# Row maxima of an attention layer: the queue from which their transfers are issued

## The chip, the cores and the metric

The kernel runs on one core of one Trainium2 chip. The metric is device time in microseconds (us), the median of several executions. Lower is better. A core has TensorE (matmuls; PE in the profile, with its weight loads as PEld), VectorE (DVE), ScalarE (ACT), GpSimd (POOL) and SyncE (SP). Each has a queue of its own that it works off in order. A transfer (DMA) is issued by an instruction in one of these queues and then carried out by 16 DMA engines.

## The reference

Four layers on a sequence of 2048 rows of 640 numbers: attention, Fourier mixing, attention, Fourier mixing, each with a layer norm ahead and a residual added.

```python
def _A_ref(x, wqkv, wo):
    B, S, D = x.shape
    H = 32; Dh = D // H; W = 256
    qkv = (lambda x, *d: x.transpose(*d))((x @ wqkv).reshape(B, S, 3, H, Dh), 2, 0, 3, 1, 4)
    q, k, v = qkv[0], qkv[1], qkv[2]
    scores = jnp.einsum("bhqd,bhkd->bhqk", q, k) * (Dh ** -0.5)
    idx = jnp.arange(S)
    mask = (idx[:, None] - idx[None, :] >= 0) & (idx[:, None] - idx[None, :] < W)
    scores = jnp.where(mask[None, None], scores, -1e9)
    p = _softmax(scores, axis=-1)
    o = jnp.einsum("bhqk,bhkd->bhqd", p, v)
    return (lambda x, *d: x.transpose(*d))(o, 0, 2, 1, 3).reshape(B, S, D) @ wo
...
x = x + _A_ref(_layernorm(x, axis=-1), A_wqkv, A_wo)
x = x + _B_ref(_layernorm(x, axis=-1), B_dft_seq_re, B_dft_seq_im, B_dft_hid_re, B_dft_hid_im)
x = x + _A_ref(_layernorm(x, axis=-1), A_wqkv, A_wo)
x = x + _B_ref(_layernorm(x, axis=-1), B_dft_seq_re, B_dft_seq_im, B_dft_hid_re, B_dft_hid_im)
```

Only the attention layers bear on the change: 32 heads of 20 numbers, each query attending to itself and the 255 keys before it.

## The kernel before, in words

The heads of a layer are worked off in eight quads of four heads. A quad has 16 blocks of 128 queries or keys, so the loop `heads` takes 8 x 16 = 128 steps, with 10 more ahead (`LEAD`). A step is made of two half steps (`z` = 0 and 1), each for two heads.

The scores are computed twice, in two orientations:

- Ahead, at step `s = t + 10`, queries stand on the partitions (`s_head`, matmul at L673). VectorE adds the mask and takes each row's maximum (L678), which goes to a small tile `mc`.
- At step `t`, keys stand on the partitions (`t_pair`, matmul at L701), so that the exponentials (`t_exp`, ScalarE, L711, into `pt`) can be multiplied with the values directly. In this orientation a row's maximum can't be subtracted by a per-partition number. It is carried by the matmul itself instead: row 60 (and row 124 for the other head of the pair) of the query tile `qp` holds minus the maximum, against a row of ones in `kp`. GpSimd then sets the masked probabilities to zero (L717, L721).

The product with the values (`pv`, L736) follows a step later, and ScalarE copies it out (L745).

Every fourth step, `m_rows` brings the maxima of four query blocks into place. I call one such unit a row block; there are 4 in a quad, 32 in a layer, 64 in the two attention layers. TensorE transposes `mc` (L686) in the second half step. ScalarE copies the result with its sign turned into `mt` (L689). Two transfers of 4 KB in all (L691), one for each `z`, write rows 60 and 124 of `qp`. The matmuls at L701 of four steps on are the first to read them. `mt` has one buffer.

The order of work is written out by hand. Every call adds an instruction to the queue of its engine, and the queue keeps that order. `post(delay, fn)` puts off a call by `delay` half steps; `tick`, at the end of every half step, makes the calls that have become due. With a delay of 1 a call is made in the tick that ends the half step in which it was posted. After the copy at L689 a half step of the steady loop adds nothing more to ScalarE's queue before that tick, and the next half step begins with its own L701 matmuls, scores (L673) and exponential (L711). In the ten steps ahead, matmuls of the projection stand between, with ScalarE's copies of their results (L586).

All transfers of the kernel are issued by SyncE (SP). In the heads these are, besides the row maxima: the parts of `qp` and `kp` for the next quad (`pack`, L636), the projected pieces to memory (`store_qk`, L566), the values (`load_v`, L663), the outputs and the sums of the probabilities (`finish`: `sm` and `o_d` at L755 and L756, `r_d` at L761), a check of the Fourier matrices (loads at L1458, a square on ScalarE at L1469), and weights.

PSUM has eight banks. The scores of both orientations, the transposed maxima and the products with the values share banks 0 to 5 by a plan made ahead (`borrow`, `borrow_pair`, with times in `AT_T`, `AT_S`, `HELD_T` and so on): a bank that an exponential empties in one half step is taken by a score matmul of the next. The matmuls between, at L274, are the projection and the output product (`fill`), a fixed number in each step.

Of the kernel before, what the change touches and what calls it, by code (L numbers as in the profile page):

```python
# [73 lines left out]
class Net:  # L74
# [573 lines left out]
    def heads(self, xsrc, xdst):  # L648
        nc = self.nc
# [33 lines left out]
        def m_rows(quad, u, bank):  # L683
            m = mc.pop((quad, u))
            p = self.banks[:16, bank, 3 * P:]
            nc.tensor.transpose(p, m.rearrange("p z e j -> p (z e j)"), self.ident)  # L686
            mt = pool.tile([16, P], F32R, name="mt", tag="mt", bufs=1)
            yield
            nc.scalar.activation(mt, p, AF.Copy, scale=-1.0)  # L689
            for z in range(2):  # L690
                self.post(1, lambda z=z: nc.sync.dma_start(  # L691
                    qp[quad % 2][60:125:64, z, u * 512:(u + 1) * 512].bitcast(F32),
                    mt[8 * z:8 * z + 8, :].bitcast(F32)))

# [123 lines left out]
        for step in range(-LEAD, steps + 1):  # L818
# [27 lines left out]
            for z in range(2):  # L846
                if 0 <= t < steps:
                    banks = self.borrow_pair(clock + AT_T[z], HELD_T)
                    t_pair(t // 16, t % 16, z, banks)
                if 0 <= s < steps:  # L850
                    for e, b in enumerate(self.borrow(clock + AT_S[z], *HELD_S)):
                        s_head(s // 16, s % 16, 2 * z + e, b)
                if z and (rows or 0 <= v < steps):
                    last, = self.borrow(clock + AT_PV, HELD_PV)
                m = m_rows(*rows, last) if z and rows else iter(())
                next(m, None)
                if 0 <= t < steps:
                    t_exp(t // 16, t % 16, z, banks)
                    t_mask(t // 16, t % 16, z)
                if self.heavy:  # L860
                    self.heavy.sort(key=lambda h: h[0] not in ROLES["m"])
                    self.relieve()
                if z:
                    if 0 <= v < steps:
                        pv(v // 16, v % 16, last)
                    for _ in m:
                        pass
                if z == 0 or t < -1 or t >= steps:
                    fill(nf)
                self.tick()  # L870
# [813 lines left out]
```

## Time and profile before

| | |
|---|---|
| median of 3 runs | 1386.3 us |
| lowest, highest | 1385.91, 1390.49 us |
| profiled execution | 1394.17 us, span 1391.8 us |
| mean granted clock of TensorE | 0.983 |
| PE busy | 1303.8 us (94%) |
| DVE busy | 965.4 us (69%) |
| ACT busy | 758.4 us (54%) |
| POOL busy | 722.3 us (52%) |
| DMA moved | 261.48 MB |

Times in the profile are counted from the start of the span. Busy times are of the one profiled execution and don't add up, since the engines work side by side. Issuing a transfer isn't counted as busy time. In a row of the timeline the first number is the start, the second the length; "x2" means two instructions merged into one row; in square brackets stands how long the engine was idle before it, and what ended that. In a row of the waits stand the total, the count and the longest. A row of a source line has the shortest, median and longest duration in ns. SPq is SyncE's queue. The first attention layer's heads run from some 147 to 530 us, the second's from some 833 to 1236.

### The profile page before, as it was taken

What the parts mean: (1) busy time and instruction counts of PE and PEld (TensorE: products, weight loads), DVE (VectorE), ACT (ScalarE), POOL (GpSimd) and SP (SyncE); (2) the same over time, 40 slices, a digit from 0 to 9 for tenths busy, and PEclk for the clock granted to TensorE, in tenths of its full rate; (3) what the DMA queues carried; (4) which work ended last, traced back from release to release, by engine and by line L of the source; (5) the groups of instructions that cost most, each with busy time, mean ns of one, the idle gap of its engine ahead of it and who ended that gap; (6) DMA issues with size and microseconds to landing.
All of it is one profiled execution on the core that took longest, in us unless ns stands there. A gap on an engine that the chain in (4) does not pass through costs nothing.

```text
span 1391.8 us, 37371 instructions
## 1 busy us (share of the span) xinstructions
PE 1303.8 (94%) x13350; PEld 1002.5 (72%) x13350; DVE 965.4 (69%) x3124; ACT 758.4 (54%) x1651; POOL 722.3 (52%) x1501
## 2 busy tenths in 40 slices
PE   6998999999998989899999999999999989999997
PEld 6898777767766767753689987777677667777445
DVE  6722788778877774777866238888688778658664
ACT  3222378767776555437422224777677755644450
POOL 4211687768777655320322136887778766733000
PEclk9999999999999999999999999999999999999999
DMA  5675567777668874617425646777776777653443
GB/s 193 206 220 168 166 204 214 203 214 213 202 207 220 234 207 134 199 54 242 171 93 184 216 151 196 216 195 224 196 225 191 235 231 209 207 157 108 140 127 144
DMA packets 174295, 261.48 MB, mean 188 GB/s; under 512 B 36306, under 2 KB 85586, under 8 KB 174100
## 3 DMA queue, kind: packets, MB, share of 16 engines
q1 hardware_dynamic: 174100, 259.00, 61.8%
q8 instruction: 108, 1.77, 0.6%
q14 instruction: 87, 0.71, 0.2%
HBM read 175.42 MB, written 82.31 MB: 185 GB/s over the span
## 4 chain that ended last, share of the span: by engine, by line
PE 36%; DMA 5%; POOL 3%; DVE 3%; issue 3%; ACT 2%; SPq 0%; POOLq 0%; ACTq 0%; DVEq 0%
PE banks L274 8%; PE banks L256 7%; PE banks L736 5%; PE banks L701 4%; PE banks L1382 3%; PE banks L673 3%; PE banks L1298 3%; PE banks L1398 1%; DMA sm<-ou 1%; ACT pt L711 1%; DMA qp<-mt 1%; DVE banks L678 1%; POOL pt L717 1%; DMA big<-x_d 1%; PE banks L362 1%
## 5 line engine op out<-in xcount | busy, mean ns | idle before, releaser
L678 DVE CUSTOM_DVE_ANT_0 banks<-banks,mask 128x384 f32<-128x384 f32 (+2 forms) x1024 | 526.8, 556 | 135.7 <-PE banks L673 115.7
L711 ACT ACTIVATE pt<-banks 128x768 f32<-128x768 f32 (+2 forms) x512 | 393.7, 770 | 162.0 <-PE banks L701 116.0
L717 POOL TENSOR_SCALAR_AFFINE_SELECT pt<-pt 128x256 f32<-128x256 f32 x512 | 218.9, 428 | 172.7 <-ACT pt L711 144.8
L274 PE MATMUL banks<-big,wc 64*128 64x512 f32 x1920 | 278.7, 400 | 0.4 <-DVE pt L480 0.4
L701 PE MATMUL banks<-qp,kp 61*128 61x384 f32 (+2 forms) x1024 | 211.0, 382 | 36.0 <-DVE mc L678 20.9
L673 PE MATMUL banks<-kp,qp 60*128 60x384 f32 (+2 forms) x1024 | 212.4, 356 | 13.3 <-DVE mc L678 9.3
L736 PE MATMUL banks<-pt,vq 128*32 128x128 f32 x5760 | 215.4, 281 | 1.2 <-ACT pt L711 0.8
L274 PEld LDWEIGHTS banks<-big,wc 64*128 64x128 f32 x1920 | 194.4, 189 | 20.4 <-ACT x L586 2.8
L721 POOL TENSOR_SCALAR_AFFINE_SELECT pt<-pt 128x256 f32<-128x256 f32 x448 | 185.9, 415 | 0.0
L736 PEld LDWEIGHTS banks<-pt,vq 128*32 128x32 f32 x5760 | 144.4, 111 | 51.7 <-issue 37.2
L701 PEld LDWEIGHTS banks<-qp,kp 61*128 61x128 f32 x1024 | 109.0, 186 | 100.6 <-DVE mc L678 71.2
L673 PEld LDWEIGHTS banks<-kp,qp 60*128 60x128 f32 x1024 | 126.0, 189 | 42.2 <-DVE mc L678 25.5
L678 DVE DVE_READ_ACCUMULATOR2_ANT mc<- 128x1 f32 x1024 | 143.6, 140 | 0.0
L1465 POOL TENSOR_TENSOR rr<-rr 128x228 f32<-128x228 f32 (+3 forms) x113 | 74.9, 667 | 87.4 <-DMA rr<-ki 34.6
L745 ACT ACTIVATE ou<-banks 128x128 f32<-128x128 f32 (+2 forms) x288 | 73.2, 266 | 66.7 <-PE banks L736 62.3
L256 PE MATMUL banks<-qp,big 128*128 128x320 f32 x576 | 99.9, 319 | 1.0 <-POOL qp L382 1.0
L228 POOL TENSOR_TENSOR c<-x,c 128x256 fp32r<-128x256 f32 x128 | 94.8, 748 | 0.0
L256 PEld LDWEIGHTS banks<-qp,big 128*128 128x128 f32 x576 | 89.8, 194 | 1.6 <-POOL qp L382 1.4
L256 PE MATMUL banks<-qp,kp 128*128 128x320 f32 x384 | 82.2, 347 | 6.9 <-ACT big L1118 4.5
L274 PE MATMUL banks<-big,big 64*128 64x320 f32 x912 | 79.6, 310 | 0.2 <-ACT mt L689 0.2
L256 PEld LDWEIGHTS banks<-qp,kp 128*128 128x128 f32 x384 | 61.0, 188 | 20.2 <-ACT big L1118 6.5
L274 PEld LDWEIGHTS banks<-big,big 64*128 64x128 f32 x912 | 72.6, 187 | 0.4 <-ACT mt L689 0.4
(169 smaller groups left out, 1746.1 us busy)
## 6 DMA issues: line engine op xcount, KB each, us to landing
qk_d<-c SPq DMA_DIRECT2D x80, 512.0 KB
kp<-qk_d SPq DMA_DIRECT2D x384, 80.0 KB
qp<-qk_d SPq DMA_DIRECT2D x384, 80.0 KB
o_d<-ou SPq DMA_DIRECT2D x64, 256.0 KB
v_d<-pt SPq DMA_DIRECT2D x16, 768.0 KB
vq<-v_d SPq DMA_DIRECT2D x64, 192.0 KB
rr<-ki SPq DMA_DIRECT2D x40, 228.0 KB
big<-x SPq DMA_DIRECT2D x26, 320.0 KB
```

The costliest lines, as they stand in the source:

```text
L228: eng.tensor_tensor(out=lo[..., c], in0=src[..., c], in1=hi[..., c].bitcast(F32), op=OP.subtract)
L256: self.nc.tensor.matmul(p, x, y, start=n == 0, stop=n == last)
L274: self.nc.tensor.matmul(ps[a], x[r], y[r], start=half + i == 0, stop=half == 1 and i == n - 1, skip_group_check=True)
L673: nc.tensor.matmul(p, qp[quad % 2][b:b + 60, z, qb * P:(qb + 1) * P], kp[quad % 2][b:b + 60, z, k0 * P:(qb + 1) * P], start=True, stop=True)
L678: nc.vector.tensor_tensor_reduce(out=p, in0=p, in1=self.mask[:, 384 - n * P:], scale=1.0, scalar=NEG, op0=OP.add, op1=OP.max, accum_out=mc ...
L701: nc.tensor.matmul(self.banks[:, banks[e], :n * P], kp[quad % 2][b:b + 61, z, kb * P:(kb + 1) * P], qp[quad % 2][b:b + 61, z, kb * P:(kb + ...
L711: nc.scalar.activation(pt[quad, kb][:, 2 * z:2 * z + 2, :n * P], self.banks[:, b0:b1 + 1, :n * P], AF.Exp, scale=SCALE)
L717: nc.gpsimd.affine_select(out=t[:, :, 0:P], in_=t[:, :, 0:P], pattern=[[0, 2], [1, P]], compare_op=OP.is_ge, fill=0.0, base=0, channel_mul ...
L721: nc.gpsimd.affine_select(out=t[:, :, 256:384], in_=t[:, :, 256:384], pattern=[[0, 2], [-1, P]], compare_op=OP.is_gt, fill=0.0, base=0, ch ...
L736: nc.tensor.matmul(self.banks[32 * h:32 * h + 32, bank, :P], vq[:, 96 * (kb % 4) + 21 * h:96 * (kb % 4) + 21 * h + 32], t[:, h, (qb - kb) ...
L745: nc.scalar.activation(ou[:, dst], self.banks[:, bank, src], AF.Copy)
L1465: eng.tensor_tensor(out=t[:, lo:hi], in0=t[:, lo:hi], in1=base.broadcast_to([P, hi - lo, w]), op=op)
```

## The change

The two transfers of a row block are issued from ScalarE's queue in place of SyncE's. The call stays posted with a delay of 1, so it stands in ScalarE's queue where the tick adds it, behind the copy at L689 and ahead of the next half step's instructions. Nothing else differs.

```diff
             nc.scalar.activation(mt, p, AF.Copy, scale=-1.0)
             for z in range(2):
-                self.post(1, lambda z=z: nc.sync.dma_start(
+                self.post(1, lambda z=z: nc.scalar.dma_start(
                     qp[quad % 2][60:125:64, z, u * 512:(u + 1) * 512].bitcast(F32),
                     mt[8 * z:8 * z + 8, :].bitcast(F32)))
```

## The prediction

> **What bounds the kernel now.** First the page (span, busy shares), then busy time by stretch inside the heads, the list of waits, and the timeline around single transfers.
>
> ```profile
> span 1391.8 us, 37371 instructions
> PE 1303.8 (94%) x13350; PEld 1002.5 (72%) x13350; DVE 965.4 (69%) x3124; ACT 758.4 (54%) x1651; POOL 722.3 (52%) x1501
> ...
> core 0: us, PE busy (x) PEld busy (x) DVE busy (x) ACT busy (x) POOL busy (x), PEclk, DMA share, GB/s
> 856.00:936.00 80.00, 79.23 (x1130) 60.30 (x1131) 66.48 (x250) 63.09 (x132) 67.52 (x154) 1.00 0.70 206
> ```
>
> In a quiet stretch of the heads PE is busy 79.23 of 80 us, and ACT, which the page calls 54% busy, is busy 63.09 of 80 there (79%). So in the heads PE sets the pace, and the others run close behind it in a ring: PE makes scores, DVE and ACT empty the banks, PE needs the banks again. A microsecond that PE waits is lost, because the order of its work is fixed.
>
> ```profile
> PE banks L701 <- DMA qp<-mt: 11.8, 7, 2.9
> ...
> PE banks L673 <- DMA kp<-qk_d: 2.4, 1, 2.4
> ...
> DVE rc L758 <- DMA sm<-ou: 5.0, 5, 2.7
> ...
> L691 SPq DMA_DIRECT2D qp<-mt x128: 503/543/959, 147.4 to 1205.9; - x128
> ...
> L689 ACT ACTIVATE mt<-banks x64: 249/250/268, 147.2 to 1205.0; 16x128 fp32r<-16x128 f32 x64
> ```
>
> There are 64 row blocks, each with one copy (L689) and two transfers (L691). PE waits for them seven times, 11.8 us in all. This is why they are late (ScalarE, SP's queue, the chain, then PE, all around one block):
>
> ```profile
> 935.46 0.25 ACT L689 ACTIVATE mt<-banks 16x128 fp32r<-16x128 f32 x1
> 935.62 0.36 ACT L711 ACTIVATE pt<-banks 128x256 f32<-128x256 f32 x1
> ...
> 937.07 1.97 SPq L636 DMA_DIRECT2D kp<-qk_d  x3
> ...
> 939.67 1.19 SPq L691 DMA_DIRECT2D qp<-mt  x2
> ...
> 939.67 4.09 DMA qp<-mt
> ...
> 943.90 0.44 PE L701 MATMUL banks<-qp,kp 61*128 61x384 f32 x2 [1.42 <-DMA qp<-mt]
> ```
>
> The copy ends at 935.71; SP, still issuing others (three for kp from 937.07 to 939.04), reaches it at 939.67; it lands 4.09 us later, and PE has stood still 1.42 us. Without the queue it would have landed about 4 us earlier, well ahead of 943.90 - 1.42 = 942.48. The late part is SP's queue, not the transfer.
>
> **The change part by part: what it gives.** The two transfers leave SP's queue and stand on ScalarE's directly behind the copy: the posted call runs in the tick that ends the same half step, and in steady steps nothing of ScalarE's comes between. From copy to landing: 0.25 us, then the first issue, 0.6 for the second and about 4 to land, some 5 us, while the block above was needed 942.48 - 935.71 = 6.8 us after the copy. The seven waits should go: 11.8 us.
>
> A long wait has a sequel: after some of them PE runs at half clock.
>
> ```profile
> 257.53 0.45 PE L701 MATMUL banks<-qp,kp 61*128 61x384 f32 x2 [1.52 <-DMA qp<-mt]
> ...
> 261.50 0.69 PE L701 MATMUL banks<-qp,kp 61*128 61x384 f32 x2
> ...
> 259.00:262.40 3.40, 3.40 (x31) 2.32 (x29) 1.66 (x7) 1.34 (x4) 2.25 (x5) 0.50 0.74 252
> ...
> 306.80:310.20 3.40, 3.40 (x29) 2.32 (x27) 1.86 (x9) 1.66 (x6) 1.53 (x4) 0.50 0.87 221
> ...
> 1081.60:1085.00 3.40, 3.40 (x27) 2.71 (x29) 1.95 (x7) 1.62 (x2) 1.92 (x5) 0.50 0.79 270
> 1146.50:1149.90 3.40, 3.40 (x38) 2.90 (x38) 1.49 (x7) 1.14 (x2) 1.51 (x4) 0.50 0.83 266
> ...
> 902.05 0.44 PE L701 MATMUL banks<-qp,kp 61*128 61x384 f32 x2
> ...
> 904.67 0.44 PE L701 MATMUL banks<-qp,kp 61*128 61x384 f32 x2
> ```
>
> A step is 2.62 us when nothing disturbs it (902.05 to 904.67) and 3.97 here (257.53 to 261.50), at clock 0.50. I price a drop at 1.7 us (1.35 in the step and an estimated 0.35 in the next). The four rows at clock 0.50 each lie within 2 us of one of the seven waits: 6.8 us.
>
> SP gives up 128 issues of 0.543 us = 69.5 us of queue. The other waits on late SP transfers above (2.4 us for kp, 5.0 us for sm) come from the same queue. I take 5 of these 7.4, and 2.5 for clock drops behind them; ends 0 and 12. What moves past SP's queue otherwise only comes earlier. Gain: 11.8 + 6.8 + 7.5 = 26 us.
>
> **What it costs.** A ScalarE instruction behind a transfer cannot start before that transfer is issued, and the transfer waits for the copy's end. Nothing is issued from ScalarE's queue in this trace, so the price comes from SP's rows: with its queue empty SP issues the pair like this.
>
> ```profile
> 147.15 0.27 ACT L689 ACTIVATE mt<-banks 16x128 fp32r<-16x128 f32 x1 [0.59 <-PE banks L686]
> ...
> 147.44 1.28 SPq L691 DMA_DIRECT2D qp<-mt  x2
> ```
>
> It starts 0.02 us behind the copy's end; two at the median of 0.543 and the small gaps between make about 1.2 us from the copy's end to ScalarE's next instruction. Call this D. Its lower end is 0 (the queue hands over and goes on); its upper end is 2.3, if each issue first waits for one of SP's. I take 1.2, since it is the same transfer.
>
> Next on ScalarE is the exponential of the next half step (L711), which today starts as the copy ends. It empties a bank that the next score matmul (L673) takes. Four blocks of one quad, copy, exponential, score matmul:
>
> ```profile
> 881.08 0.25 ACT L689 ACTIVATE mt<-banks 16x128 fp32r<-16x128 f32 x1
> 881.32 0.81 ACT L711 ACTIVATE pt<-banks 128x768 f32<-128x768 f32 x1
> ...
> 882.34 0.34 PE L673 MATMUL banks<-kp,qp 60*128 60x384 f32 x2
> ...
> 892.05 0.25 ACT L689 ACTIVATE mt<-banks 16x128 fp32r<-16x128 f32 x1
> 892.21 0.36 ACT L711 ACTIVATE pt<-banks 128x256 f32<-128x256 f32 x1
> ...
> 893.12 0.39 PE L673 MATMUL banks<-kp,qp 60*128 60x384 f32 x2
> ...
> 902.36 0.25 ACT L689 ACTIVATE mt<-banks 16x128 fp32r<-16x128 f32 x1
> 902.53 0.81 ACT L711 ACTIVATE pt<-banks 128x768 f32<-128x768 f32 x1
> ...
> 903.61 0.34 PE L673 MATMUL banks<-kp,qp 60*128 60x384 f32 x2
> ...
> 913.74 0.25 ACT L689 ACTIVATE mt<-banks 16x128 fp32r<-16x128 f32 x1
> 913.96 0.81 ACT L711 ACTIVATE pt<-banks 128x768 f32<-128x768 f32 x1
> ...
> 914.91 0.30 PE L673 MATMUL banks<-kp,qp 60*128 60x256 f32 x2
> ```
>
> In the first, the exponential ends at 882.13 and the matmul starts at 882.34: 0.21 us to spare. It would start at 881.33 + 1.2 = 882.53, 1.21 later. The bank's hand-over takes 0.05 (next fence), so PE stands 1.21 - 0.16 = 1.05 us. The others in the same way: 1.29 - 0.50 = 0.79; 1.28 - 0.22 = 1.06; 1.23 - 0.09 = 1.14. Mean 1.01. That such a delay does reach PE is seen where other work already holds ScalarE up:
>
> ```profile
> 973.47 0.80 ACT L711 ACTIVATE pt<-banks 128x768 f32<-128x768 f32 x1
> ...
> 974.32 0.19 PEld L673 LDWEIGHTS banks<-kp,qp 60*128 60x128 f32 x2 [0.47 <-ACT pt L711]
> 974.32 0.44 PE L673 MATMUL banks<-kp,qp 60*128 60x384 f32 x2 [0.21 <-ACT pt L711]
> ```
>
> The exponential ends at 974.27 and the load starts 0.05 later, after 0.47 us of idle weight loading and 0.21 of idle matmul: between 0.45 and all of such a stall is lost. I take 0.82, nearer to the load, which comes first. Of the 64 blocks the first two of each layer run before any exponential, and the eight of the last quads I count at nothing, as the heads thin out there: 52 x 1.01 = 52.5, times 0.82 = 43 us. It changes by 0.82 x 52 x 0.1 = 4.3 us with every 0.1 of D.
>
> Behind the exponential on ScalarE the second exponential of the step is pushed too, but it ends by about 0.7 us late while PE by then is 1 us behind, so it costs nothing more. VectorE and GpSimd wait for the same PE and ScalarE and lose with them.
>
> The sum: +43 - 26 = +17. The profiled execution took 1394.17 us (span 1391.8), 7.9 above the median 1386.3, so its like would be about 1411 and the median 1403.
>
> The Trainium skill, "TensorE: Matmul & The Clock Gate", section "Why this matters for your kernels", says to avoid idle gaps above some 3 us, since a window of idleness halves the clock. Here a gap of 1.52 us was followed by clock 0.50, so the trace does not agree with that length; by the page the new 1 us stalls never touch the clock, and by the trace that is likely but not sure (rival four).
>
> **The rivals.**
> One, the other side: issue is short on ScalarE. The cost equals the gain where 43 - 43 x (1.2 - D) = 26, at D = 0.80. For this: no row shows ScalarE's own issue. Against: SP's 128 rows never fall under 0.503 us. At D = 0.3 no margin but 0.05 to 0.25 us a block is left to pay, 6 us at most: -20, 1366.
> Two: the two queues get in each other's way. At D = 1.75, half of the pairs' possible wait, the cost is 43 + 24 = 67: +41, 1427; at 2.3, 43 + 47 = 90: +64, 1450. For it: SP's rows around the late block follow one another closely, from 937.07 to 940.86. Against: nothing here shows two issuers.
> The Trainium skill, "Perfetto Trace Analysis", section "DMA Instruction — HWDGE (DVE, Sync)", says that a sequencer must lock a shared descriptor generator, and that the wait counts in the issue's shown time. No run here shows it yet; by that rule this rival holds.
> Three: the rows still come late (the landing on the other queue takes over 6 us), so 18.6 of the gain stays away: +36, 1422. Against: 4.09 us above, from a full queue.
> Four: the new stalls bring clock drops. One in five of 52 would be 10 x 1.7 = 17 us more: 1420. Against: the four drops above follow waits of 1.52 us and more, and the wait of 1.42 us has none behind it.
>
> **How the numbers follow.** Forecast (D 1.0 to 1.45; 1394 to 1414) 0.50; one 0.22, from 1366 to 1390; two 0.16; three 0.05; four 0.07. The predicted time is 1403. From 1374 to 1440 leaves out about half of rival one's and the end of two's: 2 in 10. The likeliest one's own range, with 0.45 to 1 of the stall lost, is 1384 to 1414. Under 0.3% (4.2 us) this measurement tells nothing. Faster: most of one and the low end of the forecast, 0.23; within 0.3%: 0.13; slower: 0.64.
>
> **What the profile after would show.** L691 on ScalarE's queue, about 0.54 us each; no wait of L701 for qp<-mt; each steady block's L711 about 1.2 us behind the copy's end; L673 waiting for ACT pt L711 near 1 us a block, the largest new row of the waits; SP's other transfers issued earlier; fewer stretches at clock 0.50. The prediction is wrong if the gap from copy to exponential is under 0.8 us, or if it is 1.2 and L673 does not wait.

## The result, and the profile after

| | before | after |
|---|---|---|
| median, same chip | 1388.39 us (1385.91 to 1391.22, 4 runs) | 1508.83 us (1505.76 to 1513.9, 4 runs) |
| profiled execution, span | 1391.8 us | 1503.6 us |
| mean granted clock | 0.983 | 0.973 |

The changed kernel is slower: ratio 1.0844, 95% interval 1.081 to 1.0879. That is +120 us where +17 was forecast, and 69 us above the end of the range. The direction was right, and the size was not.

All of it is lost in the heads: from the first to the last L701 they take 438 us in each of the two layers, after 383 and 380. The page of after, and busy time in a stretch of the heads:

```profile
span 1503.6 us, 37124 instructions
PE 1346.0 (90%) x13350; PEld 1019.8 (68%) x13350; DVE 971.2 (65%) x3124; ACT 758.5 (50%) x1651; POOL 719.3 (48%) x1501
...
core 0: us, PE busy (x) PEld busy (x) DVE busy (x) ACT busy (x) POOL busy (x), PEclk, DMA share, GB/s
180.00:260.00 80.00, 72.08 (x972) 53.24 (x971) 57.14 (x215) 53.91 (x114) 56.98 (x128) 0.99 0.60 178
```

In before, PE was busy 79.45 of 80 us from 170 to 250 and 75.33 of 80 from 250 to 330, with a granted clock of 0.96 there. Here it has eight idle microseconds, at almost full clock. No other engine is full: ACT and GpSimd each fall below 58 of 80. So something that this table doesn't list holds them all.

The list of waits (total us, count, longest us):

```profile
POOL rr L1465 <- DMA rr<-ki: 64.5, 23, 7.9
...
PEld banks L673 <- ACT pt L711: 57.6, 69, 1.9
...
POOL rr L1465 <- DMA rr<-kr: 50.0, 20, 5.4
...
DVE rc L758 <- DMA sm<-ou: 41.6, 28, 3.5
...
PE banks L673 <- ACT pt L711: 38.2, 58, 1.6
...
PE banks L673 <- DVE mc L678: 28.9, 25, 3.2
...
PE banks L736 <- POOL pt L717: 10.1, 12, 1.6
PE banks L673 <- DMA qp<-qk_d: 9.2, 2, 5.2
```

The same rows of before, as far as it has them:

```profile
POOL rr L1465 <- DMA rr<-ki: 34.6, 12, 8.0
...
POOL rr L1465 <- DMA rr<-kr: 15.0, 11, 3.5
...
PE banks L673 <- DVE mc L678: 9.3, 9, 3.1
...
PE banks L673 <- ACT pt L711: 1.5, 7, 0.2
```

The row that was forecast is there (L673 waits for ACT pt L711, 38.2 us), and the wait of L701 for the row maxima (11.8 us) is gone. But others that the prediction doesn't name have grown with it: GpSimd waits for the loads of the Fourier check, VectorE for `sm` (5.0 us before), PE for VectorE's maxima. GpSimd and VectorE wait there for SP's own transfers, which were said to come earlier. They come later, and the waits of SP's queue say why:

```profile
SPq L636 <- DMA qp<-mt: 101.4, 44, 4.3
...
SPq L636 <- DMA kp<-qk_d: 61.2, 106, 2.3
...
SPq L663 <- DMA qp<-mt: 33.6, 13, 4.6
...
SPq L755 <- DMA qp<-mt: 18.3, 7, 7.1
```

The two largest rows of before in which a load (L636) waits for an earlier load:

```profile
SPq L636 <- DMA qp<-qk_d: 14.6, 35, 1.1
...
SPq L636 <- DMA kp<-qk_d: 9.0, 28, 0.7
```

SP stops before transfers that have nothing to do with the row maxima (parts of `qp` and `kp`, values, sums) until a transfer of the row maxima, which is no longer its own, has landed. With the smaller rows of L906 and L1458 (9.1 and 6.5 us) that is 168.9 us in 69 places by this list of after. In before SP has no row for `qp<-mt`, and L636 waits 9.0 us for `kp<-qk_d`, where it is 61.2 in after.

One such stop, from ScalarE's and SP's queues of after:

```profile
220.59 0.25 ACT L689 ACTIVATE mt<-banks 16x128 fp32r<-16x128 f32 x1
220.88 1.07 ACTq L691 DMA_DIRECT2D qp<-mt  x2
...
219.86 4.43 SPq L636 DMA_DIRECT2D qp<-qk_d  x3
```

Three issues that need 0.3 us each take 4.43. Here are the same instructions and their neighbours, listed from the trace with the semaphore that each transfer raises when it lands, and when its last part landed:

```
issued  us    queue  transfer        semaphore  landed
212.46  0.56  SP     sm<-ou          100        215.43
213.64  0.38  SP     r_d<-rc         102        217.46
...
219.86  0.29  SP     qp<-qk_d        107        223.85
220.52  0.29  SP     qp<-qk_d        108        224.04
220.88  0.52  ACT    qp<-mt          100        224.00
221.43  0.52  ACT    qp<-mt          102        224.18
224.02  0.27  SP     qp<-qk_d        100        226.78
224.39  0.35  SP     vq<-v_d         101        227.71
224.78  0.36  SP     qp<-qk_d        102        228.22
```

All transfers of SP and ScalarE in this program share eight semaphores (100 to 105, 107, 108). They are handed out in turn over both queues, in the order of the program as it was built, and each transfer first waits until the one before it on its semaphore has landed. I call such a place in the turn a slot. While all were on SP's queue the order of the turn was also the order of issue. Now SP passes over ScalarE's two, issues the ones written after them, and then meets their semaphores. It is done with 108 at 220.81, ScalarE doesn't reach the pair until 220.88, and SP starts 0.02 us after the landing at 224.00: 3.2 us in which its whole queue stands. Counted from the trace there are 50 such stops in the heads of after, 118.0 us, in which SP issues directly (within 0.06 us) after the landing of ScalarE's transfer on its next semaphore. The list has 51 us more, since before loads of values and stores of sums (L663, L755) the wait for the semaphore is an instruction of its own, just ahead of the transfer: 18 stops, 47 us. Counts of stops below are of the first kind. In before all transfers are SP's own, and it stands some 65 us in such stops, each for an earlier one of its own (after: some 116 us of these too).

### The profile page after: what moved, and what is told of

Its sections match the earlier page's. It is cut to its first block, busy times and chain, and to the rows that moved or that the text cites. A ratio compares the mean times of both kernels' runs of the same rounds, so it can differ in the third digit from the quotient of the medians.

```text
span 1503.6 us, 37124 instructions
## 1 busy us (share of the span) xinstructions
PE 1346.0 (90%) x13350; PEld 1019.8 (68%) x13350; DVE 971.2 (65%) x3124; ACT 758.5 (50%) x1651; POOL 719.3 (48%) x1501
## 4 chain that ended last, share of the span: by engine, by line
PE 32%; DMA 7%; DVE 3%; ACT 3%; issue 3%; POOL 2%; ACTq 1%; SPq 1%; DVEq 0%; POOLq 0%
PE banks L274 7%; PE banks L256 6%; PE banks L736 4%; PE banks L673 3%; PE banks L1382 3%; PE banks L1298 3%; PE banks L701 3%; ACT pt L711 2%; DMA sm<-ou 2%; DVE banks L678 1%; DMA rr<-ki 1%; ACTq L691 1%; PE banks L1398 1%; DMA qk_d<-c 1%; DMA kp<-qk_d 1%
## 5 line engine op out<-in xcount | busy, mean ns | idle before, releaser
L711 ACT ACTIVATE pt<-banks 128x768 f32<-128x768 f32 (+2 forms) x512 | 390.3, 771 | 210.3 <-PE banks L701 105.0
L717 POOL TENSOR_SCALAR_AFFINE_SELECT pt<-pt 128x256 f32<-128x256 f32 x512 | 219.1, 429 | 210.0 <-ACT pt L711 189.4
L673 PE MATMUL banks<-kp,qp 60*128 60x384 f32 (+2 forms) x1024 | 233.6, 365 | 77.3 <-ACT pt L711 38.2
L274 PE MATMUL banks<-big,wc 64*128 64x512 f32 x1920 | 281.9, 403 | 0.4 <-DVE pt L480 0.4
L701 PE MATMUL banks<-qp,kp 61*128 61x384 f32 (+2 forms) x1024 | 213.7, 386 | 26.4 <-DVE mc L678 23.8
L736 PE MATMUL banks<-pt,vq 128*32 128x128 f32 x5760 | 221.5, 282 | 17.6 <-POOL pt L717 10.1
L673 PEld LDWEIGHTS banks<-kp,qp 60*128 60x128 f32 x1024 | 130.5, 190 | 128.0 <-ACT pt L711 57.6
L701 PEld LDWEIGHTS banks<-qp,kp 61*128 61x128 f32 x1024 | 111.1, 189 | 90.8 <-DVE mc L678 69.0
L274 PE MATMUL banks<-big,big 64*128 64x320 f32 x912 | 85.5, 324 | 0.2 <-ACT mt L689 0.2
L274 PEld LDWEIGHTS banks<-big,big 64*128 64x128 f32 x912 | 77.6, 199 | 0.4 <-ACT mt L689 0.4
```

Source lines behind the costliest of these rows:

```text
L274: self.nc.tensor.matmul(ps[a], x[r], y[r], start=half + i == 0, stop=half == 1 and i == n - 1, skip_group_check=True)
L673: nc.tensor.matmul(p, qp[quad % 2][b:b + 60, z, qb * P:(qb + 1) * P], kp[quad % 2][b:b + 60, z, k0 * P:(qb + 1) * P], start=True, stop=True)
L701: nc.tensor.matmul(self.banks[:, banks[e], :n * P], kp[quad % 2][b:b + 61, z, kb * P:(kb + 1) * P], qp[quad % 2][b:b + 61, z, kb * P:(kb + ...
L711: nc.scalar.activation(pt[quad, kb][:, 2 * z:2 * z + 2, :n * P], self.banks[:, b0:b1 + 1, :n * P], AF.Exp, scale=SCALE)
L717: nc.gpsimd.affine_select(out=t[:, :, 0:P], in_=t[:, :, 0:P], pattern=[[0, 2], [1, P]], compare_op=OP.is_ge, fill=0.0, base=0, channel_mul ...
L736: nc.tensor.matmul(self.banks[32 * h:32 * h + 32, bank, :P], vq[:, 96 * (kb % 4) + 21 * h:96 * (kb % 4) + 21 * h + 32], t[:, h, (qb - kb) ...
```

## The experiments

Ratios and differences are against the kernel before, measured beside each run on the same chip. In the expectations, theory R is that the shared semaphores cost most and ScalarE's stall some 45 us; theory S is that the stall alone makes the whole loss.

**e2_none: the gain alone.**

```diff
-            for z in range(2):
+            for z in range(2 if quad < 2 else 0):
```

> The pair is left out from the third quad of each layer on (later quads use the maxima of the first two, so the computation is changed there); nothing takes its place. This measures what the transfers cost on SP's queue, the gain term of the prediction: 26 us by its working for all 64 blocks, 12 quads of 16 here. Both theories: 15 to 30 us faster than before. If the lateness on SP's queue was of no consequence: within 10 us of before.

Measured: 1366.64 us, ratio 0.979 (0.9727 to 0.9854), -26 us against 1392.73. The prediction's gain was 26 for all 64 blocks; here 48 of them go without the pair, so that in proportion all would give some 35 (an estimate). The gain is not the term that failed.

**e4_pool: the pair from the third queue.**

```diff
-                self.post(1, lambda z=z: nc.sync.dma_start(
+                self.post(1, lambda z=z: nc.gpsimd.dma_start(
```

> The pair issued from GpSimd's queue. ScalarE is free of it, SP too. Theory R: GpSimd's transfers should not take part in SP's eight semaphores, so SP has no waits for the pair and runs ahead of before; what is left is GpSimd's own time for issuing, not seen in any run yet: -20 us if it is below 0.5 us a transfer, +20 to +60 if it is 1 us and more, since GpSimd is 84% busy in the heads. Theory S: the same range, as ScalarE is not stalled.

Measured: 1400.93 us, ratio 1.0035 (1.0003 to 1.0067), +8 us, between the two ends that were expected.

```profile
L691 POOL DMA_DIRECT2D qp<-mt x128: 541/557/754, 147.0 to 1212.6; - x128
...
DMA to landing us min/median/max: 1.8/4.1/7.2
```

Here the issues are as long as SP's were (median 557 ns against 543), the landing takes longer than from ScalarE (median 4.1 us against 2.25 in after), and yet it costs 8 us over before and not 120. SP's list has no row for `qp<-mt`; in the trace GpSimd's transfers raise semaphores of their own (111 to 118). A second queue is therefore not by itself what costs.

**e5_later: ScalarE's stall taken away, the transfers kept on ScalarE.** The pair is posted half a step later, so the exponential goes first.

```diff
-                self.post(1, lambda z=z: nc.scalar.dma_start(
+                self.post(2, lambda z=z: nc.scalar.dma_start(
```

> As the changed kernel, but posted with a delay of 2, so that the pair stands in ScalarE's queue behind the first exponential of the next step instead of ahead of it, where ScalarE has some 0.5 us of idle time before the next exponential. The stall of PE should fall from 1.0 to some 0.4 us a block. Theory R: SP still has to wait for ScalarE's landing, so the loss falls by 20 to 35 us only, to some +85 to +100 over before, SP's waits for the pair as long as in the changed kernel (150 us and more). Theory S: the loss falls with the stall, to +20 to +50.

Measured: 1503.92 us, ratio 1.0806 (1.0733 to 1.0879), +111 us: above the +85 to +100 of theory R, and far above the +20 to +50 of theory S.

```profile
DVE rc L758 <- DMA sm<-ou: 68.0, 31, 4.6
PE banks L673 <- DVE mc L678: 48.0, 30, 3.8
...
PE banks L673 <- ACT pt L711: 4.1, 19, 0.3
```

PE's wait for the exponential falls from 38.2 to 4.1 us, and the time stays within 1%. Whatever costs 111 us isn't the exponential that starts late. The rows that hang on SP grow in its place, so the two costs don't simply add; SP's stops stay (117.2 us in 52, 118.0 in 50 in after).

**e1_copies, e1_copies_later, e1_four, e1_four_later: ScalarE's time alone.** The pair stays on SP. Small copies to a scratch tile stand where the change put the pair (delay 1), or half a step later (delay 2).

```diff
+            def idle():
+                scr = pool.tile([16, 64], F32, name="scr", tag="scr", bufs=1)
+                for _ in range(10):      # e1_four, e1_four_later: 4
+                    nc.scalar.activation(scr, self.ident[:16, :64], AF.Copy)
+            self.post(1, idle)           # ..._later: 2
```

> SP issues the pair as in the kernel before; in the place where the changed kernel issues it, ScalarE gets ten small copies (16 x 64) into a tile that nobody reads, about 1.1 us, and no transfer. Theory R (ScalarE's stall is one cost, some 45 us; the larger one is that transfers of both queues use eight semaphores in turn, so SP must stop until ScalarE's transfer has landed): +30 to +55 us over before, no stops of SP of that kind, the exponential about 1.1 us behind the copy. Theory S (the stall alone makes the loss): +100 us or more.

> The same ten copies posted with a delay of 2, behind the next exponential, the place of the pair in the run with the later post. Theory R: the stall is mostly covered there, 0 to +20 us over before, so that of the +111 of the later post some 100 belong to the transfers being transfers. Theory S: +80 us or more, as that run lost 111.

The ten copies missed the dose: they hold ScalarE for 2.82 us, not for the pair's 1.1. Measured 1565.96 us, ratio 1.1238 (1.1153 to 1.1323), +177 us, and later 1513.65, ratio 1.0861 (1.0801 to 1.0921), +125. They don't answer the question, but give a second point. Four copies have the right length:

> As the run with ten copies at the place of the pair, but four. The ten took 2.8 us, not 1.1, and cost 177 us; four should take 1.1 to 1.2 us and match the 1.15 us for which the pair holds ScalarE. Theory R: what the pair costs as ScalarE time, 40 to 70 us over before (43 by the prediction's working, the rest by more stretches at half clock). Theory S (the time alone makes the whole loss): 100 to 145 us over before, since here SP keeps its 26 us of cost as well.

> The four copies posted with a delay of 2, the place of the pair in the run with the later post (+111) and of the two further transfers (+148). Theory R: 0 to +30 us over before, so 80 us and more of those losses come from the transfers standing among SP's. Theory S: +90 us or more.

Measured: 1397.93 us, ratio 1.0056 (1.003 to 1.0082), and 1398.21, ratio 1.0072 (1.0042 to 1.0102): +9 us each. At the place of the pair that is far below what either theory expected (40 to 70, and 100 to 145); half a step later it lies in the range of theory R. ScalarE's queue and PE's waits of e1_four (L717 is the exponential there):

```profile
196.23 0.25 ACT L689 ACTIVATE mt<-banks 16x128 fp32r<-16x128 f32 x1
196.38 1.10 ACT L698 ACTIVATE scr<-ident 16x64 f32<-16x64 f32 x4
197.39 0.78 ACT L717 ACTIVATE pt<-banks 128x768 f32<-128x768 f32 x1
...
PE banks L673 <- ACT pt L717: 20.2, 46, 0.6
...
PE banks L707 <- DMA qp<-mt: 1.8, 2, 1.6
```

From the copy's end (196.48) to the exponential are 0.91 us, and PE waits 20.2 us for it. In after this gap is 1.15 us (195.92 to 197.07 around one block, next section) and the wait 38.2. So an occupied ScalarE of nearly this length costs some 10 us net, not 120. Part of what it takes comes back at once: PE waits for the row maxima in two places instead of seven (1.8 us, 11.8 before), and it runs at half clock for 26 us instead of 50.

**e9_extra and e17_extra_pool: the same additional transfers, once on ScalarE, once on GpSimd.** The pair stays on SP. Two transfers of 2 KB of `mt` to a scratch tile are added, with a delay of 2, so that the exponential goes first.

```diff
+            scr = pool.tile([16, 64], F32R, name="scr", tag="scr", bufs=1)
+            for z in range(2):
+                self.post(2, lambda z=z: nc.scalar.dma_start(     # e17_extra_pool: nc.gpsimd
+                    scr[8 * z:8 * z + 8, :].bitcast(F32), mt[8 * z:8 * z + 8, :64].bitcast(F32)))
```

> SP issues the pair as before, and ScalarE issues two further transfers a block (2 KB each, into a tile that nobody reads), posted with a delay of 2. Against the copies at that place this adds only that transfers from a second queue stand among SP's. Theory R: SP stops for them as in the later post and has its own issues of the pair besides, +90 to +160 us over before, SP's waits for transfers from ScalarE 100 us and more. Theory S, or any theory in which only moving the pair matters: as the copies at that place, within 25 us of them.

> The twin of e9: SP issues the pair as in the kernel before, and the two dummy transfers of 2 KB of mt to a scratch tile are issued from GpSimd instead of ScalarE. Theory of the shared semaphores (transfers of SP and ScalarE take turns on the same eight, those of GpSimd have their own): SP shows no more than 15 us of stops for the dummies, and the time is 0 to +15 us against before (two issues of about 0.56 us a block on GpSimd, which is half idle). Rival (the additional transfers do the harm themselves, by the DMA engines or by holding mt longer): near the +148 us that the same dummies cost from ScalarE, at least +60.

Measured: from ScalarE 1537.09 us, ratio 1.105 (1.0972 to 1.1129), +148 us; from GpSimd 1409.84, ratio 1.0177 (1.0127 to 1.0227), +22 us, somewhat above the 15 that was expected at most, and far under the rival's 60. SP's list in e9_extra:

```profile
SPq L636 <- DMA scr<-mt: 67.5, 29, 3.9
SPq L759 <- DMA scr<-mt: 52.1, 20, 4.3
```

With smaller rows that is 147.0 us. In e17_extra_pool SP has no row for `scr<-mt`. What follows at PE, first in e9_extra, then in e17_extra_pool (L705 is here the matmul that reads the row maxima):

```profile
PE banks L705 <- DMA qp<-mt: 71.0, 30, 4.3
```

```profile
PE banks L705 <- DMA qp<-mt: 8.4, 7, 2.2
```

The pair, which SP issues in both, comes late behind SP's stops. Nothing was moved off SP in either, nobody reads `scr`, and the bytes are the same. Some 126 us hang on the queue that issues them. It isn't ScalarE's time: in e9_extra PE's L673 waits 3.9 us for the exponential, and four copies half a step later cost 9 us.

**e3_one: one transfer of each pair on ScalarE, one on SP.**

```diff
-                self.post(1, lambda z=z: nc.sync.dma_start(
+                self.post(1, lambda z=z: (nc.sync if z else nc.scalar).dma_start(
```

> Of each pair the first transfer goes from ScalarE and the second from SP, both with a delay of 1. By ScalarE's time alone: one issue holds it for about 0.6 us from the copy's end, less than the 0.91 us of four copies (+9 us), so 0 to +10 us. By the shared semaphores: a slot of ScalarE's still comes in every block, so SP stops in most blocks, 40 to 120 us of stops in all, and the time is +40 to +100 us. If it grew in proportion to the number of slots it would be near +55.

Measured: 1495.2 us, ratio 1.0807 (1.0742 to 1.0871), +107 us, just above what the shared semaphores were expected to cost, and far from the 0 to 10 of ScalarE's time.

```profile
195.79 0.25 ACT L689 ACTIVATE mt<-banks 16x128 fp32r<-16x128 f32 x1
196.07 0.51 ACTq L691 DMA_DIRECT2D qp<-mt  x1
196.62 0.81 ACT L711 ACTIVATE pt<-banks 128x768 f32<-128x768 f32 x1 [0.58 <-PE banks L673]
```

```profile
PE banks L701 <- DMA qp<-mt: 21.8, 16, 3.2
...
PE banks L673 <- ACT pt L711: 7.1, 25, 0.4
```

ScalarE gives up 0.58 us instead of 1.15, and the exponential holds PE for 7.1 us instead of 38.2; the time hardly falls. Halving the transfers doesn't halve the cost, since one slot in a block stops SP as well as two do: 46 stops, 126.9 us. And the half that SP still issues comes late again (21.8 us).

**e16_lump and e16_lump_before: SP given more to do ahead.** The loads of the next quad's parts come twelve at a time instead of three, so that SP would lie behind ScalarE and find the slots already landed; e16_lump is that on top of e5_later, e16_lump_before is that on the kernel before.

```diff
-                    defer(i // 3, f)
+                    defer(i // 12, f)
```

> The later post on ScalarE, and the twelve loads of a part of the next quad (L636) issued together in the step of the row block in place of three a step. Then SP has some 12 transfers to issue around the pair's place in the order, lies behind it, and reaches the transfers that take the pair's semaphores only after the pair has landed. Theory R: SP's waits for the pair fall from over 150 us to under 50, and the loss from +111 to +20 to +60. Theory S: unchanged, within 15 us of the later post, or slower.

> The control for the run with the loads together: the same change of the order on the kernel before, all transfers on SP. The pair stands behind the lump and lands later, so both theories expect 0 to +40 us over before, and no gain that could explain a fall of the loss in the other run.

Measured: 1490.28 us, ratio 1.0732 (1.0664 to 1.08), +102 us, a miss; the control 1385.63, ratio 0.9993 (0.9961 to 1.0025).

```profile
SPq L636 <- DMA qp<-mt: 72.4, 34, 4.3
```

The loads' grouping is worth nothing by itself, and SP still ran into ScalarE's slots, partly at other lines of its queue (150 us in all, where under 50 were expected). The idea that SP could be kept behind in this way was wrong. Taken alone the time is what theory S expected here; since the stops that were to go are still there, the run tells nothing for or against the cause.

**e12_store: SP relieved by another transfer.** The stores of the projected pieces (L566) go from GpSimd in the heads; the pair stays on SP.

```diff
-        self.nc.sync.dma_start(
+        (self.nc.sync if self.slot is None else self.nc.gpsimd).dma_start(
```

> A candidate for a better version, with the row maxima on SP as before: in the heads the stores of the projected pieces (64 transfers, L566) are issued from GpSimd's queue, which writes these pieces, in place of SP's. SP gives up 64 issues of 0.39 us and the stops in which it waits for GpSimd's result with everything behind it (44 us over the kernel). If SP's lateness is what costs, as both theories have it for the kernel before: 5 to 20 us faster than before. If GpSimd's time for issuing (0.56 us each, 36 us in all) reaches the critical chain: same or up to 15 us slower.

Measured: 1383.87 us, ratio 0.9966 (0.9931 to 1.0), -5 us. It is the fastest kernel here that computes everything, but its interval touches 1, so that it beats the kernel before isn't shown.

## Why the prediction was right or wrong, point by point

**The gain, 26 us: right as far as tested.** Without the pair in 48 of the 64 blocks there are 26 us less. In after no L701 waits for `qp<-mt`.

**D, 1.2 us from the copy's end to the exponential: right.** The timeline and the issues of after:

```profile
195.67 0.25 ACT L689 ACTIVATE mt<-banks 16x128 fp32r<-16x128 f32 x1
195.96 1.07 ACTq L691 DMA_DIRECT2D qp<-mt  x2
197.07 0.81 ACT L711 ACTIVATE pt<-banks 128x768 f32<-128x768 f32 x1 [1.15 <-PE banks L274]
...
L691 ACTq DMA_DIRECT2D qp<-mt x128: 502/517/1136, 146.6 to 1316.0; - x128
```

1.15 us, with a median of 0.517 us for an issue where 0.543 was taken from SP. Rival one (a short issue) is out.

**The stall, 43 us: right in size.** PE waits for the exponential 38.2 us in 58 places, the weight load 57.6 in 69; forecast were 52.5 us of stall and 43 of loss in 52 places. What it costs in time can only be estimated. For the 0.91 us of e1_four the formula gives 43 - 2.9 x 4.3 = 31, and +9 was measured, with 10 us of the waits for row maxima and 24 us of half clock (worth some 12 by the prediction's price) already gone. That is about the prediction's 11.8 + 6.8, so this part of the gain can't be taken off again. With the formula's step for the longer gap, +9 + 2.4 x 4.3 = +19 is then an upper estimate of what after would have cost without SP's stops, near the +17 on record.

**"What moves past SP's queue otherwise only comes earlier": this step failed.** SP's relief was put at +7.5 us, with ends of 0 and 12, so a loss was left out altogether. The two transfers didn't leave SP's order: they kept their two places in the turn of the eight semaphores, and SP now waits there for another engine. It gave up 69.5 us of issuing and got 168.9 us of stops (118.0 by the narrower count), and behind them its transfers land late, VectorE and GpSimd stand in their order before them, and PE waits for both. The chain of the work that ended last shows it in the heads of the second layer: its parts on `DMA sm<-ou` grow from 10.8 to 24.1 us, those on `DMA rr<-ki` from 0 to 12.7. With ScalarE's stall taken away (e5_later) the coupling leaves +111 although the pair is off SP's queue there too, so it costs over 100 us. Neither of the two signs that the prediction named for being wrong came about: both watched ScalarE, and none watched SP's queue.

The trace of before could have told it. Its SP waits of `L636 <- DMA qp<-qk_d` (14.6 us, 35) and `<- DMA kp<-qk_d` (9.0, 28) are waits of a load for earlier loads that it doesn't read (some 65 us of SP's stops before are waits for a slot); an issue that waits for an unrelated landing is a sign of a shared slot, and asking which slots the moved transfers hold was the missing question.

**Rival two, the queues get in each other's way: right in words, wrong in mechanism.** It priced a longer D, up to 2.3, for which 1.15 stands above. The landings of the pair became shorter too (median 2.75 to 2.25 us). The rule of the Trainium skill that was cited with it ("Perfetto Trace Analysis", section "DMA Instruction — HWDGE (DVE, Sync)": the wait for a shared, locked descriptor generator counts in the issue's shown time) isn't borne out: with two issuers the median is 0.517 us on ScalarE, also for the 39 issues of 128 that overlap one of SP's, and was 0.543 on SP alone. The Trainium skill, "DMA: Bandwidth & Descriptors", section "Issuing engines are not separate DMA queues", says that issuing from several engines only saves the time on the sequencer; the trace agrees on what is saved (69.5 us of SP's issuing), but what is lost, SP's stops, is over twice that by SP's list (168.9 us). The same page of the Trainium skill, section "Why a DMA increments its semaphore by 16 and not by 1", advises one semaphore for each in-flight slot, because two transfers in flight on one semaphore can satisfy each other's waits. The stop at 220.81 is how this program keeps to that with eight: it waits for the earlier landing. Here the slots' price at ScalarE's transfers is 168.9 us by SP's list (118.0 by the narrower count) once they belong to two queues.

**Rival three, rows still late: out.** No wait for them in after.

**Rival four, clock drops from new stalls: drops came, but hardly from the stalls that it meant.** Clock records of the traces, added up: half clock for 50 us in 12 stretches before, 85 in 18 in after, 26 in e1_four, 129 in e5_later, 174 in e9_extra. The two runs in which PE hardly waits for the exponential (e5_later 4.1 us, e9_extra 3.9) have the most, and e1_four, with 20.2 us, has the least; so in these runs the drops come with the coupling. At the prediction's price, 1.7 us for a stretch of 3.4, the 35 us more are some 17 of the 120 (an estimate). The forecast of fewer such stretches was wrong.

**What stays open.** PE's idle time grew from 88.0 to 157.6 us and its busy time from 1303.8 to 1346.0. How much of the second is half clock and how much comes of how overlapping matmuls are recorded isn't settled. Nor was a version run in which ScalarE's transfers have semaphores of their own; GpSimd's, which have, stand in for it. They differ in more than that: the profile lists them on a queue `software_dynamic`, those of SP and ScalarE on queues `hardware_dynamic`. That the semaphores are what costs therefore rests on SP's stops, read from the traces, together with the times.

## What to carry to other kernels

Before a transfer is moved to another queue, look at what it shares with those that stay: if completion semaphores are handed out in turn over several queues, a queue that runs ahead stops when it meets a slot that the other hasn't used yet, and everything behind it lands late. The sign in a profile is an issue that waits for the landing of a transfer which it doesn't read; price that wait for the whole queue, not for the one transfer. To separate an engine's time from its transfers, put compute of the same length in their place (+9 us here), and the same transfers on a queue with slots of its own (+22 against +148).

## What the runs showed of the hardware that was not expected

ScalarE's time costs far more than in proportion to its length. 1.10 us of copies in each row block cost 9 us in all, 2.82 us cost 177:

```profile
198.78 2.82 ACT L698 ACTIVATE scr<-ident 16x64 f32<-16x64 f32 x10
...
PE banks L673 <- ACT pt L717: 119.6, 63, 2.4
```

PE's wait grows by 99.4 us, the time by 168. With it half clock goes from 26 us to 208 us in 44 stretches, and the mean granted clock from 0.992 to 0.935; half of the 182 us more is 91, enough for the 69 that the waits leave open. The first twenty stretches of e1_copies (3.41 or 6.83 us each) all start within 2.5 us of a PE wait of 1.58 to 3.2 us, while e1_four's waits for the exponential are 0.6 us at most. Over the whole of e1_copies half clock begins within 2 us at 40 of the 60 PE waits of 1.5 us and more, and at 2 of the 57 from 0.3 to 1.5 us. That the four small copies are cheap because their waits stay short fits this; a length between 1.10 and 2.82 us was not run.
